# Attention with routed experts on one core: first scores ahead of the branch, a new order for stretches without expert work, new durations in the plan

## The chip, the cores and the metric

The kernel runs on one core of a Trainium2 chip. The metric is the device time of one execution in microseconds (us), the median over runs. TensorE (PE in the rows, PEld for its weight loads) multiplies matrices, ScalarE (ACT) does tanh and exponential, VectorE (DVE) the elementwise work and the casts, GpSimd (POOL) small fills and indirect transfers, and SyncE (SP) issues most DMA transfers. About 1%, 4.6 us here, is what a measurement of this kernel can tell from no change.

## What is computed

Attention over 8 batches, 12 heads, 448 places and head size 64 with capped scores, then a routed expert layer on the 128 best places of each batch:

```python
scores = scale * q @ k.T                    # (448 x 448 for each head)
scores = cap * tanh(scores / cap)           # cap = 30
attn   = softmax(scores);  x = attn @ v     # heads side by side: (8, 448, 768)

s = x[b] @ w_gate                           # for each batch b
top = the 128 places with the largest s     # each goes through the expert
out[b] = x[b]
out[b, top] += sigmoid(s[top]) * (relu(x[b, top] @ w1) @ w2)   # 768 -> 1024 -> 768
```

Everything is float32. Where more speed is wanted, a factor is split into a high and a low part and the product is made of three.

## The kernel before

The 96 heads are done four at a time, in 24 "doubles"; three doubles make a batch. A double has four units, three of 128 keys and a last one of 64. A unit of **scores** (`scores_mm`, L476) is 16 matmuls (12 where the parts are split, from the fifth double on) into the one score buffer `psS` of four PSUM banks. ScalarE takes the tanh out of `psS` into one of four `p` buffers (L911) and then the exponential in place (L918). A unit of **values** (`values_mm`, L507) is 56 matmuls from `p` and `v` into `psV`, the only accumulator, of two banks. After the last unit of a double VectorE evacuates `psV` (`evac`, L538 to L544), and the result is stored and scored for the gate (L573). The two short last units of two neighbouring doubles share one unit of scores.

When a batch has its three doubles, **selection** (`select_proc`, L589) adds the gate scores (L600), writes them to a line in DRAM (`put`, L611), reads the line back broadcast to all 128 partitions (`get`, L614), joins its tail (`sums`, L618), ranks all places by comparisons (L640, L648), makes one-hot columns (L677), and turns them into indices on TensorE (L687). A gather fetches the rows (L703, POOL), and the **expert** follows: transposes (L732), first layer, relu (L817), transposes, second layer (both L778, matmul by matmul), combination (L832), scatter (L839). Picks, transposes and both layers take the one bank pair `psT` (`K.banks`). Each selection begins behind its own batch, so that expert work is there only in some stretches.

The order of all this is worked out when the kernel is built. `Sim` holds a clock for each engine; every `Task` has an engine, a duration in ns, what it depends on and a priority, and is emitted in the order that the plan gives. On the chip each engine then goes through its instructions in that order and waits for semaphores. On TensorE `Front.policy` (L1002) chooses between Q (scores), V (values) and F (expert work): if a run of four units of values is ready, or one that continues such a run (`run_ready`), the order of choice is V, Q, F, otherwise Q, F, V. A choice that can start within 170 ns is taken, else the one that starts first. `LATE` adds time to the planned landing of the broadcast row before `sums` is placed in VectorE's order.

Ahead of a branch on the cap (L1280), `load_flag` (L319) loads the cap, makes an identity on POOL, warms TensorE up with seven products of it and tests the cap, and `first_loads` (L1148) starts the loads of the first double on SP. Loads and the flag stand outside the planned part; the fast path behind the branch is the planned one.

Of the kernel before, what the change touches and what calls it, by code (L numbers as in the profile page):

```python
# [16 lines left out]
P = 128  # L17
HD = 64
CAP_FAST = 40.0
EPS = 1e-9  # L20
WARM = 7
HALF = (slice(0, HD), slice(HD, 2 * HD))
# [3 lines left out]

LATE = 3000

# [290 lines left out]
def load_flag(tc, K, cap):  # L319
    nc = tc.nc  # L320
    nc.sync.dma_start(K.cap, cap.to_broadcast([P, 1]))
    make_identity(nc, K.ident)
# [38 lines left out]
def weights_proc(tc, K, w1, w2):  # L361
# [17 lines left out]
    for n, (nm, w, i, m) in enumerate(parts):  # L379
# [5 lines left out]
            hi, st[:, :m]), deps=[land], reads=[src], prio=K.wprio, kind="whi"))  # L385
        b = sim.add(Task("DVE", m * 1.05 + 70, lambda t, hi=hi, lo=lo, st=st, m=m:
                         nc.vector.tensor_tensor(lo, st[:, :m], hi.bitcast(F32),
# [87 lines left out]

def scores_mm(tc, K, D, c, i):  # L476
    full = K.NCH - 1
    if D.parts and c < full:
        (kh, kl), (qh, ql) = ([part[nm].slots[0].obj for part in (D.high, D.low)] for nm in "kq")
        terms = ((kh, qh), (kh, ql), (kl, qh))  # L480
        for r in range(2):
            for n, (a, b) in enumerate(terms):
                for j in range(2):
                    tc.nc.tensor.matmul(K.S4[:, 2 * r + j, :K.S],  # L484
                                        lhsT=a[HALF[j], r, c * P:(c + 1) * P],
                                        rhs=b[HALF[j], r, :], start=(n == 0), stop=(n == 2))
        return
    k, q = D.at("k"), D.at("q")
    for r in range(2):
        for h in range(2 if c < full else 1):  # L490
            for j in range(2):
                half, n = (h, 2 * r + j) if c < full else (r, 2 * i + j)
                at = c * P + h * HD
                tc.nc.tensor.matmul(K.S4[HALF[half], n, :K.S], lhsT=k[HALF[j], r, at:at + HD],  # L494
                                    rhs=q[HALF[j], r, :], start=True, stop=True)
# [27 lines left out]
def output_proc(tc, K, D):  # L523
# [24 lines left out]
    for r in range(2):  # L548
        e = Task("DVE", 790, lambda t, r=r: evac(t, r), deps=[D.values] + out,
                 take=[K.rec] if r else [K.rec, K.xn, K.xt],  # L550
# [38 lines left out]
def select_proc(tc, K, b):  # L589
# [20 lines left out]
    def put(t):  # L610
        nc.sync.dma_start(t.slots[0].obj.rearrange("o (p c) -> (o p) c", c=NCH), score)  # L611

    def get(t):
        nc.sync.dma_start(t.slots[0].obj, ln.obj.to_broadcast([P, NCH * P]))  # L614

    def sums(t):
# [6 lines left out]

    w = yield Task("SP", 700, put, deps=[t], take=[K.line], refs=[1], reads=[sc], lag=900, prio=0,
                   kind="put")
    ln = w.slots[0]
    r = yield Task("SP", 700, get, deps=[w], take=[K.row], refs=[2 * NCH], reads=[ln], lag=900,
                   prio=0, kind="get")
    rs = r.slots[0]
    row = rs.obj  # L630
    places = row.rearrange("p (a c) -> p a c", c=NCH)
    r = yield Task("DVE", 600, sums, deps=[(r, LATE)], reads=[sc], prio=1, kind="joined")
    r = [r]
    k = yield Task("DVE", 0, lambda t: None, take=[K.rk], refs=[2], prio=1, kind="none")
    rk = k.slots[0]
    todo = []
    for c in range(NCH):
        def greater(t, c=c):
# [4 lines left out]
        def ties(t, c=c):  # L643
# [7 lines left out]

        todo.append(sim.add(Task("DVE", 820, greater, deps=r, reads=[rs, sc], prio=PG,
                                 kind="greater")))
        todo.append(sim.add(Task("DVE", 430 + 110 * c, ties, deps=r, reads=[rs, sc], prio=PG,
                                 kind="ties")))
# [9 lines left out]
    for n in range(chunks):  # L665
# [3 lines left out]
        def one_hot(t, s0=s0):  # L669
            sel = t.slots[0].obj  # L670
            for c in range(NCH):
# [4 lines left out]
                else:  # L676
                    nc.vector.tensor_scalar(sel[:, c, :], K.iota, rk.obj[:, 2, c:c + 1], None,  # L677
                                            op0=ALU.is_equal)

        o = yield Task("DVE", 790, one_hot, deps=[rank], take=[K.sel], refs=[1],  # L680
                       reads=[rk] if n == chunks - 1 else [], prio=1, kind="onehot")
# [166 lines left out]
class Front:  # L848

    def __init__(self, tc, K, Ds):  # L850
# [19 lines left out]
        NB = K.B  # L870
        self.total = NB * 18800
        self.over = False

    def score_est(self):
# [14 lines left out]
    def score_task(self):  # L889
# [18 lines left out]
        def soft(_):  # L908
# [13 lines left out]
            self.S_free = th.start + 1768 + 60  # L922
            e = yield Task("ACT", 1690, exp, deps=[th], prio=3, kind="exp")
            for D, c in two:
# [77 lines left out]
    def policy(self):  # L1002
# [18 lines left out]
        seg = self.seg  # L1021
        run = self.run_ready(t)
        if run:
            order = "VQF"
        elif True:
            order = "QFV"
        else:
            order = "QVF"
        kind = None
# [4 lines left out]
        if kind is None:  # L1034
            wait = {"Q": 0, "V": 0, "F": PATIENCE}
            kind = min(start, key=lambda k: start[k] + wait[k])
        return self.commit(start[kind], f[1] if kind == "F" else None, kind, shapes[kind],
                           kind == "F" and seg != "F")

    def run_ready(self, t):  # L1040
# [106 lines left out]

def first_loads(tc, K, D):  # L1148
    nc = tc.nc
    for nm, src, ring in (("q", K.qd, K.q), ("k", K.kd, K.k), ("v", K.vd, K.v)):  # L1150
# [4 lines left out]
        setattr(D, nm, ev)  # L1155
    q, k = D.at("q"), D.at("k")
    nc.sync.dma_start(k[:, :, :2 * HD], K.kd[D.d][:, :, :2 * HD])
    for r in range(2):
        nc.sync.dma_start(q[:, r], K.qd[D.d][:, r])
    nc.sync.dma_start(k[:, :, 2 * HD:], K.kd[D.d][:, :, 2 * HD:])  # L1160
    nc.sync.dma_start(D.at("v"), K.vd[D.d])
    ones(tc, D.v, D.v)


# [97 lines left out]
def main_kernel(ctx: ExitStack, tc: tile.TileContext, q, k, v, cap, w_gate, w1, w2, out, C, dims):  # L1262
# [11 lines left out]
    K.const = ctx.enter_context(tc.tile_pool(name="const", bufs=1))  # L1274
    allocate(tc, K)
    load_flag(tc, K, cap)
    first = Double(K, 0)
    first_loads(tc, K, first)
    fast = nc.values_load(K.fast[0:1, 0:1], min_val=0, max_val=1)
# [58 lines left out]
```

## Time and profile before

| what | us |
|---|---|
| median of 3 runs (lowest to highest) | 457.3 (454.99 to 459.11) |
| the profiled execution | 458.26 |
| its span, first to last instruction | 456.5 |
| TensorE busy in the span | 431.3 (94%) |
| ScalarE busy | 303.0 (66%) |
| VectorE busy | 276.1 (60%) |
| GpSimd busy | 23.6 (5%) |

The rows come from the profiled execution. Times are microseconds from the start of the span. A matmul's end is modelled, so a busy TensorE is not one at its peak. In square brackets of a row stands how long the engine was idle before it, and what ended that.

### The profile page before, as it was taken

Reading aid. Unit: us, or ns where it says so; the run is one execution under the profiler, and the core shown is the slowest. Engines: PE = TensorE matmul, PEld = TensorE weight load, DVE = VectorE, ACT = ScalarE, POOL = GpSimd, SP = SyncE. Lnnn points to the kernel's source line nnn. Section 1 sums busy time; section 2 is a strip of 40 time slices with the busy share of each in tenths; the row PEclk is TensorE's granted clock in tenths of the full one; section 3 lists DMA queues with packets and bytes.
Section 4 is the critical chain, followed back from the end, with each engine's and each line's share of the span. In section 5 each row is a group of like instructions: output and inputs, shape, how many; then the busy total and the mean of one; then the engine's idle time right before and its main releaser. Section 6 shows DMA issues by size and latency. Waiting matters only on the chain.

```text
span 456.5 us, 17936 instructions
## 1 busy us (share of the span) xinstructions
PE 431.3 (94%) x8126; PEld 360.5 (79%) x8126; DVE 276.1 (60%) x847; ACT 303.0 (66%) x191; POOL 23.6 (5%) x55
## 2 busy tenths in 40 slices
PE   6999889999999999999999999999999799999993
PEld 4665566778889788898788988789888689878893
DVE  0176789965963874847657695479455832476211
ACT  4889989895895785876499498597678696011000
POOL 1000000100000000000000020000010000100010
PEclk9899999999999999999999999999999899999999
DMA  7977396462353532623254453522732201401011
GB/s 229 369 235 257 112 288 202 159 226 86 114 168 90 192 106 86 227 74 118 59 190 118 151 163 108 184 87 84 233 123 67 84 3 42 137 1 36 2 71 41
DMA packets 34197, 60.75 MB, mean 133 GB/s; under 512 B 11200, under 2 KB 21184, under 8 KB 34112
## 3 DMA queue, kind: packets, MB, share of 16 engines
q1 hardware_dynamic: 32832, 53.22, 35.9%
q0 software_dynamic: 1280, 6.29, 4.2%
q8 instruction: 66, 1.08, 0.9%
q14 instruction: 19, 0.16, 0.1%
HBM read 45.33 MB, written 14.17 MB: 130 GB/s over the span
## 4 chain that ended last, share of the span: by engine, by line
PE 80%; ACT 7%; DMA 5%; issue 3%; DVE 3%; SPq 1%; POOL 0%; DVEq 0%; POOLq 0%; ACTq 0%
PE psV L507 27%; PE psT L778 22%; PE psS L484 16%; PE psS L494 7%; ACT p L911 4%; PE psA L778 4%; ACT p L918 2%; PE psB L778 2%; DMA row<-line 1%; PE psT L732 1%; DMA xe<-out,idx 1%; DMA k<-in_k 1%; ACT plent L911 1%; DMA out<-p,idx 1%; DMA q<-in_q 1%
## 5 line engine op out<-in xcount | busy, mean ns | idle before, releaser
L911 ACT ACTIVATE p<-psS,sc 128x1792 f32<-128x1792 f32 x63 | 110.3, 1750 | 63.8 <-PE psS L494 34.2
L507 PEld LDWEIGHTS psV<-v,p 128*64 128x64 f32 (+1 forms) x3864 | 106.0, 139 | 23.4 <-issue 11.6
L507 PE MATMUL psV<-v,p 128*64 128x65 f32 (+1 forms) x3864 | 113.5, 225 | 5.9 <-issue 2.0
L918 ACT ACTIVATE p<-p,capc 128x1792 f32<-128x1792 f32 x63 | 112.9, 1793 | 1.7
L484 PE MATMUL psS<-qh,kh 64*128 64x448 f32 x240 | 49.1, 405 | 2.3 <-ACT p L911 2.1
L911 ACT ACTIVATE plent<-psS,sc 128x1792 f32<-128x1792 f32 x21 | 36.8, 1752 | 14.4 <-PE psS L484 7.7
L538 DVE RECIPROCAL rec<-psV 128x7 f32<-128x7 f32 x48 | 9.6, 200 | 60.0 <-PE psV L507 49.8
L494 PE MATMUL psS<-q,k 64*64 64x448 f32 x328 | 37.3, 569 | 3.9 <-ACT p L911 2.7
L918 ACT ACTIVATE plent<-plent,capc 128x1792 f32<-128x1792 f32 x21 | 37.6, 1793 | 0.7
L507 PEld LDWEIGHTS psV<-v,plent 128*64 128x64 f32 (+1 forms) x1288 | 34.8, 137 | 4.1 <-issue 2.7
L507 PE MATMUL psV<-v,plent 128*64 128x65 f32 (+1 forms) x1288 | 37.7, 223 | 0.3 <-issue 0.2
L573 DVE CUSTOM_DVE_ANT_0 jk<-xn,wg 128x256 bf16<-128x256 f32 x72 | 30.4, 422 | 1.3
L484 PEld LDWEIGHTS psS<-qh,kh 64*128 64x128 f32 x240 | 22.8, 185 | 9.0 <-ACT p L911 4.5
L539 DVE TENSOR_TENSOR xn<-psV,rec 128x384 f32<-128x384 f32 x48 | 26.8, 558 | 1.9 <-DVE rec L538 0.3
L453 DVE CAST kh<-k 128x896 fp32r<-128x896 f32 x20 | 12.5, 624 | 22.8 <-PE psS L484 22.8
L640 DVE TENSOR_SCALAR_CACHE_REDUCE jk<-row,score 128x512 bf16<-128x512 f32 (+1 forms) x32 | 23.7, 740 | 0.8
L494 PEld LDWEIGHTS psS<-q,k 64*64 64x64 f32 x328 | 11.8, 138 | 15.6 <-issue 9.0
L484 PE MATMUL psS<-ql,kh 64*128 64x448 f32 x120 | 22.3, 366 | 0.0
L778 PE MATMUL psT<-w2h,hh 64*128 64x384 f32 x192 | 21.3, 345 | 1.0 <-DVE xl L748 0.4
L484 PE MATMUL psS<-qh,kl 64*128 64x448 f32 x120 | 22.1, 363 | 0.0
L484 PE MATMUL psS<-qlent,kh 64*128 64x448 f32 x120 | 21.9, 362 | 0.0
L484 PE MATMUL psS<-qh,klent 64*128 64x448 f32 x120 | 21.9, 362 | 0.0
(149 smaller groups left out, 604.9 us busy)
## 6 DMA issues: line engine op xcount, KB each, us to landing
v<-in_v SPq DMA_DIRECT2D x23, 455.0 KB, 3.7
q<-in_q SPq DMA_DIRECT2D x22, 448.0 KB, 4.8
k<-in_k SPq DMA_DIRECT2D x22, 448.0 KB, 5.7
out<-xn SPq DMA_DIRECT2D x24, 384.0 KB, 3.5
stage<-in_moe_w SPq DMA_DIRECT2D x4, 512.0 KB, 6.0
row<-line SPq DMA_DIRECT2D x8, 256.0 KB, 3.9
stage<-in_moe_w SPq DMA_DIRECT2D x5, 384.0 KB, 3.2
out<-xt SPq DMA_DIRECT2D x48, 32.0 KB, 3.1
```

Source lines behind the costliest of these rows:

```text
L453: nc.vector.tensor_copy(t.slots[0].obj, self.at(nm))
L484: tc.nc.tensor.matmul(K.S4[:, 2 * r + j, :K.S], lhsT=a[HALF[j], r, c * P:(c + 1) * P], rhs=b[HALF[j], r, :], start=(n == 0), stop=(n == 2))
L494: tc.nc.tensor.matmul(K.S4[HALF[half], n, :K.S], lhsT=k[HALF[j], r, at:at + HD], rhs=q[HALF[j], r, :], start=True, stop=True)
L507: tc.nc.tensor.matmul(D.acc.obj[HALF[g], r, i * WIDE:(i + 1) * WIDE], lhsT=p[rows, h, n * HD:(n + 1) * HD], rhs=v[rows, u, :], start=(c == ...
L538: nc.vector.reciprocal(rec, blocks[:, :, K.D])
L539: nc.vector.tensor_tensor(slots[0].obj.rearrange("p c (r j d) -> p r j c d", r=2, j=2)[:, r], blocks[:, :2 * full, :K.D].rearrange("p (j c ...
L573: nc.vector.tensor_tensor_reduce(out=K.jk[:, :x.shape[1]], in0=x, in1=g, scale=1.0, scalar=0.0, op0=ALU.mult, op1=ALU.add, accum_out=part[ ...
L640: nc.vector.tensor_scalar(K.jk[:m], row[:m], score[:m, c:c + 1], None, op0=ALU.is_gt, op1=ALU.add, accum_out=rk.obj[:m, 0, c:c + 1])
L732: nc.tensor.transpose(t.slots[0].obj[:, h, i * HD:(i + 1) * HD], src()[half, i * P:(i + 1) * P], K.ident[half, half])
L778: ins = nc.tensor.matmul(bank.obj[:, g, :width], lhsT=pair.obj[part][HALF[h], i, :], rhs=K.wts[r][HALF[h], i, g * width:(g + 1) * width], ...
L911: nc.scalar.activation(slot.obj, K.S4[:, :, :K.S], AF.Tanh, scale=K.sc)
L918: nc.scalar.activation(slot.obj, slot.obj, AF.Exp, scale=K.cap)
```

## The change

The cap's load moves into `first_loads`, which now runs ahead of `load_flag`; half of q is loaded from ACT's queue. `first_scores` issues the first unit of scores ahead of the branch into the two bank pairs `K.acc` and `K.banks`, which are idle then. `Front.begin` plans the first tanh in two parts (one for each pair), its exponential, and ten small matmuls behind the tanh. The policy gets a test, `backlog`: if no expert product is ready within 1000 ns, the order of choice depends on what was done last (after scores F, V, Q; after values Q, F, V; after expert work V, Q, F). `put` and `get` of the first batch go to GpSimd's queue with planned costs of 1000 and 2800 ns and no `LATE`; `LATE` is halved for the others. Several planned durations are set anew, and the comparisons of the last selection get a higher priority.

```diff
-WARM = 7
+WARM, KEEP = 7, 10
-LATE = 3000
+LATE = 1500
+THIN_Q, THIN_V, THIN_F = "FVQ", "QFV", "VQF"
+SOON = 1000
+LINE, LATER, FIRST = ("POOL", 1000, 2800, "gpsimd"), ("SP", 700, 900, "sync"), 1
...
 def load_flag(tc, K, cap):
-    nc.sync.dma_start(K.cap, cap.to_broadcast([P, 1]))
...
-        b = sim.add(Task("DVE", m * 1.05 + 70, lambda t, hi=hi, lo=lo, st=st, m=m:
+        b = sim.add(Task("DVE", m * 1.05 + 145, lambda t, hi=hi, lo=lo, st=st, m=m:
...
-def scores_mm(tc, K, D, c, i):
+def scores_mm(tc, K, D, c, i, banks=None):
+    if banks is None:
+        banks = [K.S4[:, n] for n in range(4)]
...
-        e = Task("DVE", 790, lambda t, r=r: evac(t, r), deps=[D.values] + out,
+        e = Task("DVE", 1030, lambda t, r=r: evac(t, r), deps=[D.values] + out,
...
+    eng, busy, lag, queue = LINE if b < FIRST else LATER
+    queue = getattr(nc, queue)
...
-    r = yield Task("DVE", 600, sums, deps=[(r, LATE)], reads=[sc], prio=1, kind="joined")
+    r = yield Task("DVE", 860, sums, deps=[(r, LATE if eng == "SP" else 0)], reads=[sc], prio=1, kind="joined")
+    pg = .5 if K.tail else PG
...
-        o = yield Task("DVE", 790, one_hot, deps=[rank], take=[K.sel], refs=[1],
+        o = yield Task("DVE", 1000, one_hot, deps=[rank], take=[K.sel], refs=[1],
...
+    def begin(self):
+        K, sim, nc = self.K, self.sim, self.tc.nc
+        D, c = self.work[0][0]
+        self.u = 1
+        pairs = [r.free.pop() for r in (K.acc, K.banks)]
+        for s in pairs:
+            s.refs = 1
+        def tanh(t):
+            for r, s in enumerate(pairs):
+                nc.scalar.activation(t.slots[0].obj[:, 2 * r:2 * r + 2], s.obj[:, :, :K.S], AF.Tanh,
+                                     scale=K.sc)
+            D.P[c], D.pslot[c] = t.slots[0].obj, t.slots[0]
+        def exp(t):
+            x = th.slots[0].obj
+            nc.scalar.activation(x, x, AF.Exp, scale=K.cap)
+        def warm(t):
+            for _ in range(KEEP):
+                nc.tensor.matmul(t.slots[0].obj[:, 0, :HD], lhsT=K.ident[HALF[0]],
+                                 rhs=K.ident[HALF[0], :HD], start=True, stop=True)
+        th = sim.add(Task("ACT", 2000, tanh, take=[K.p], refs=[1], reads=pairs, prio=0,
+                          kind="tanh"))
+        D.exp[c] = sim.add(Task("ACT", 1740, exp, deps=[th], prio=0, kind="exp"))
+        w = Task("PE", KEEP * 111, warm, deps=[th], take=[K.banks], refs=[1], prio=(0, 0),
+                 kind="warm")
...
-            e = yield Task("ACT", 1690, exp, deps=[th], prio=3, kind="exp")
+            e = yield Task("ACT", 1740, exp, deps=[th], prio=3, kind="exp")
...
-        run = self.run_ready(t)
-        if run:
-            order = "VQF"
-        elif True:
-            order = "QFV"
+        if not self.backlog(t, SOON):
+            order = THIN_Q if seg == "Q" else THIN_V if seg == "V" else THIN_F
         else:
-            order = "QVF"
+            order = "VQF" if self.run_ready(t) else "QFV"
...
+    def backlog(self, t, within):
+        for task in self.sim.pend["PE"]:
+            if task.kind in ("open", "mm"):
+                if task.kind == "open" and self.K.open >= 1:
+                    continue
+                r = task.ready()
+                if r is not None and r <= t + within:
+                    return True
+        return False
...
-def first_loads(tc, K, D):
+def first_loads(tc, K, D, cap):
...
+    nc.scalar.dma_start(q[:, 0], K.qd[D.d][:, 0])
+    nc.sync.dma_start(K.cap, cap.to_broadcast([P, 1]))
     nc.sync.dma_start(k[:, :, :2 * HD], K.kd[D.d][:, :, :2 * HD])
-    for r in range(2):
-        nc.sync.dma_start(q[:, r], K.qd[D.d][:, r])
+    nc.sync.dma_start(q[:, 1], K.qd[D.d][:, 1])
     nc.sync.dma_start(k[:, :, 2 * HD:], K.kd[D.d][:, :, 2 * HD:])
     nc.sync.dma_start(D.at("v"), K.vd[D.d])
     ones(tc, D.v, D.v)
+
+def first_scores(tc, K, D):
+    pairs = K.acc.slots[0].obj, K.banks.slots[0].obj
+    scores_mm(tc, K, D, 0, 0, [b[:, n] for b in pairs for n in range(2)])
+    for s in (D.q, D.k):
+        s.slots[0].refs -= 1
...
+    first = Double(K, 0)
+    first_loads(tc, K, first, cap)
     load_flag(tc, K, cap)
-    first = Double(K, 0)
-    first_loads(tc, K, first)
+    first_scores(tc, K, first)
     fast = nc.values_load(K.fast[0:1, 0:1], min_val=0, max_val=1)
```

## Rows read from the trace of the kernel before

**Rows 1.** Page, busy us (share of the span) and instructions of each engine.

```profile
PE 431.3 (94%) x8126; PEld 360.5 (79%) x8126; DVE 276.1 (60%) x847; ACT 303.0 (66%) x191; POOL 23.6 (5%) x55
```

**Rows 2.** Windows: start:end, length, busy us by engine; last granted clock, DMA share, GB/s.

```profile
0.00:20.00 20.00, 16.26 (x190) 9.81 (x190) 1.01 (x8) 12.00 (x8) 3.30 (x18) 0.91 0.85 292
20.00:100.00 80.00, 73.13 (x1636) 53.38 (x1634) 63.39 (x170) 74.01 (x45) 1.91 (x6) 1.00 0.67 220
100.00:350.00 250.00, 246.28 (x4836) 212.97 (x4834) 164.69 (x510) 186.30 (x115) 12.44 (x24) 1.00 0.41 130
350.00:370.00 20.00, 17.41 (x424) 14.93 (x422) 15.45 (x55) 12.91 (x10) 0.13 (x1) 0.91 0.16 49
370.00:450.00 80.00, 78.24 (x1054) 69.43 (x1053) 30.81 (x105) 17.79 (x18) 4.84 (x5) 1.00 0.14 42
450.00:456.50 6.50, 0.00 (x0) 0.00 (x0) 0.76 (x2) 0.00 (x0) 0.96 (x1) 0.83 0.18 67
```

**Rows 3.** Timeline 0 to 15 us: start, us, engine, line, operation.

```profile
0.81 0.39 SPq L321 DMA_DIRECT2D capc<-in_cap  x1
1.42 3.35 PE L325 MATMUL psT<-ident 128*128 128x128 f32 x14 [1.42 <-POOL ident masks.py:199]
2.01 1.06 SPq L1159 DMA_DIRECT2D q<-in_q  x2
3.64 0.14 DVE L328 RECIPROCAL sc<-capc 128x1 f32<-128x1 f32 x1
3.75 0.14 DVE L327 TENSOR_SCALAR fast<-sq 1x1 int32<-1x1 f32 x1
5.08 2.70 PE L494 MATMUL psS<-q,k 64*64 64x448 f32 x16 [0.30 <-DMA q<-in_q]
7.90 1.75 ACT L911 ACTIVATE p<-psS,sc 128x1792 f32<-128x1792 f32 x1 [3.77 <-PE psS L494]
9.23 0.12 POOL L473 MEMSET v<- 128x14 f32 x1 [7.86 <-DMA v<-in_v]
9.69 1.79 ACT L918 ACTIVATE p<-p,capc 128x1792 f32<-128x1792 f32 x1
9.71 2.54 PE L494 MATMUL psS<-q,k 64*64 64x448 f32 x16 [1.92 <-ACT p L911]
12.32 1.75 ACT L911 ACTIVATE p<-psS,sc 128x1792 f32<-128x1792 f32 x1 [0.84 <-PE psS L494]
```

**Rows 4.** A window at the start, columns as in rows 2.

```profile
9.70:12.20 2.50, 2.49 (x18) 0.65 (x18) 0.53 (x3) 1.78 (x1) 2.07 (x7) 0.66 0.99 378
```

**Rows 5.** The chain that ended last: start, us, what it was.

```profile
25.59 1.73 PE psS L494 x16
...
263.63 0.97 PE psV L507 x56
...
349.93 6.03 PE psV L507 x224
...
360.82 1.29 issue
...
373.69 1.78 PE psV L507 x56
```

**Rows 6.** Timeline of ScalarE: a wait for scores.

```profile
32.27 1.76 ACT L911 ACTIVATE p<-psS,sc 128x1792 f32<-128x1792 f32 x1 [1.30 <-PE psS L494]
```

**Rows 7.** Selection: timeline of SP and VectorE, and the page's issue of the gathers.

```profile
57.80 0.69 SPq L611 DMA_DIRECT2D line<-score  x1
60.02 0.55 DVE L384 CAST w2h<-stage 128x768 fp32r<-128x768 f32 x1
71.07 0.28 DVE L618 TENSOR_TENSOR row<-row 128x64 f32<-128x64 f32 x1
...
253.11 0.28 DVE L618 TENSOR_TENSOR row<-row 128x64 f32<-128x64 f32 x1 [1.61 <-DMA row<-line]
...
xe<-out,idx POOLq DMA_INDIRECT x6, 4.6
```

More of the change, by code (lines that the diff above doesn't have):

```diff
@@ L483, in scores_mm @@
                 for j in range(2):
-                    tc.nc.tensor.matmul(K.S4[:, 2 * r + j, :K.S],
+                    tc.nc.tensor.matmul(banks[2 * r + j][:, :K.S],
                                         lhsT=a[HALF[j], r, c * P:(c + 1) * P],
@@ L493, in scores_mm @@
                 at = c * P + h * HD
-                tc.nc.tensor.matmul(K.S4[HALF[half], n, :K.S], lhsT=k[HALF[j], r, at:at + HD],
+                tc.nc.tensor.matmul(banks[n][HALF[half], :K.S], lhsT=k[HALF[j], r, at:at + HD],
                                     rhs=q[HALF[j], r, :], start=True, stop=True)
@@ L610, in put @@
     def put(t):
-        nc.sync.dma_start(t.slots[0].obj.rearrange("o (p c) -> (o p) c", c=NCH), score)
+        queue.dma_start(t.slots[0].obj.rearrange("o (p c) -> (o p) c", c=NCH), score)
     def get(t):
-        nc.sync.dma_start(t.slots[0].obj, ln.obj.to_broadcast([P, NCH * P]))
+        queue.dma_start(t.slots[0].obj, ln.obj.to_broadcast([P, NCH * P]))
     def sums(t):
@@ L622, in sums @@
                                        accum_out=score[:HD, last:])
-    w = yield Task("SP", 700, put, deps=[t], take=[K.line], refs=[1], reads=[sc], lag=900, prio=0,
+    eng, busy, lag, queue = LINE if b < FIRST else LATER
+    queue = getattr(nc, queue)
+    w = yield Task(eng, busy, put, deps=[t], take=[K.line], refs=[1], reads=[sc], lag=lag, prio=0,
                    kind="put")
     ln = w.slots[0]
-    r = yield Task("SP", 700, get, deps=[w], take=[K.row], refs=[2 * NCH], reads=[ln], lag=900,
+    r = yield Task(eng, busy, get, deps=[w], take=[K.row], refs=[2 * NCH], reads=[ln], lag=lag,
                    prio=0, kind="get")
@@ L650, in ties @@
                                            accum_out=rk.obj[:m, 1, c:c + 1])
-        todo.append(sim.add(Task("DVE", 820, greater, deps=r, reads=[rs, sc], prio=PG,
+        todo.append(sim.add(Task("DVE", 820, greater, deps=r, reads=[rs, sc], prio=pg,
                                  kind="greater")))
-        todo.append(sim.add(Task("DVE", 430 + 110 * c, ties, deps=r, reads=[rs, sc], prio=PG,
+        todo.append(sim.add(Task("DVE", 430 + 110 * c, ties, deps=r, reads=[rs, sc], prio=pg,
                                  kind="ties")))
@@ L871, in __init__ @@
         self.total = NB * 18800
+        self.begin()
         self.over = False
+    def begin(self):
[22 more added lines that the diff above has]
+                 kind="warm")
+        w.reads.append(lambda: w.slots[0])
+        sim.add(w)
     def score_est(self):
```

## The prediction

> **What bounds the kernel now.** I read the page's busy shares first. TensorE is busy 94% of the span, no other engine over 66% [rows 1]. So the question is where the missing 25.2 us lie. The table of windows answers it: TensorE is idle 3.7 us of the first 20, 6.9 us between 20 and 100, 3.7 us in the 250 between 100 and 350, 2.6 us between 350 and 370, 1.8 us between 370 and 450, and all of the last 6.5 us, where only the last combination and scatter run [rows 2]. A change of order can win only from those holes, and the last 6.5 us is not touched by it.
>
> Then the timeline of the start. The first scores wait for q (issued third on SP) until 5.08, the first tanh starts at 7.90, and the second scores wait until that tanh has left the one score buffer, 9.71 [rows 3]. TensorE does nothing for 1.92 us ahead of them, and in the stretch that follows the granted clock is 0.66 on average, between its two levels of 1.2 and 2.4 GHz, so that 16 matmuls take 2.54 us where the same 16 take 1.73 later [rows 3, 4, 5]. ScalarE, which feeds everything in this stage, starts its second tanh at 12.32.
>
> Between 20 and 100 both engines are nearly full: ScalarE 74.0 of 80 us, TensorE 73.1 [rows 2]. Here the chain of waits jumps between them. Where two units of values stand together, the next scores come late and ScalarE waits 1.30 us [rows 6]. The same happens at about 59 and 85 us, so there are three such places. The worst place is at 350: four units of values in a row take 6.03 us, in which ScalarE gets no scores, and soon after TensorE itself waits 1.29 us because no exponential is ready [rows 5].
>
> **The change, part by part.** *First scores ahead of the branch.* Half of q is issued on ACT, so it need not wait behind the cap and k on SP: q was issued at 2.01 and its first half was there at 5.08, 3.1 us later [rows 3]. Issued near 0.9 (SP's own first transfer goes out at 0.81) it lands at about 4.0, before TensorE has ended its 14 warming matmuls at 1.42 + 3.35 = 4.77 [rows 3]. The first 8 matmuls then run from 4.8 to about 5.7. The other half of q moves one place forward and is there at about 5.0, so the second 8 end near 6.7. Tanh in two parts: half of 1.75 us with some 0.1 for the second start, so it runs 5.8 to 7.8, and the exponential of 1.79 to 9.6. The second scores go to the score buffer, which nobody holds. They need the rest of k, which is issued earlier than before, and they run about 6.8 to 8.6. So the second tanh starts at 9.6 where it started at 12.32: **-2.7 us**. At worst q and k land as before; then only the split tanh and the free buffer count: second part of tanh from 7.9 to 8.8, exponential to 10.6, -1.7. At best the lost clock does not fall either, which is 2.54 - 1.73 = 0.8 more: -3.5. The ten small matmuls put behind the second scores stand in a time in which TensorE waits for the exponential, so I cost them at nothing; without that cover they are some 1 us (the plan's own 111 ns each).
>
> *Scores first where no expert work is ready.* In thin stretches the new order alternates scores and values, where the old one took values as long as they were ready. No work goes away. Bounded by the holes: between 20 and 100 from 0 to -6.9 us of idle TensorE, and the three late scores are 1.30 us of ScalarE each. Since both engines are nearly full there, I take half of three such waits, **-1.9**. At 350 the expert's first layer has just ended and its second is not ready, so the run of four would be broken up and the 1.29 us wait filled: **-1.3** (0 to -2.6, the hole of that window). Between 100 and 350: **-0.6** of the 3.7 us. The price is more changes of array shape: one large unit alone takes 1.78 on the chain, a small one 0.97, so three large and one small are 6.31 where a run of the four takes 6.03, which is 0.09 for each joint [rows 5]. I count 35 joints in the timeline of values, 9 of them in thin stretches: **+0.8** (if all 35 break, +3.2).
>
> *First selection on POOL's queue.* Between the issue of the score line (57.80) and the first use of the returned row (71.07) lie 13.3 us [rows 7]. The plan now has 2 times (1000 + 150 + 2800 ns) = 7.9 us, so the first expert starts about 5 us earlier beyond the shift. Nothing of TensorE's work is saved; experts only fill time in which TensorE is idle 6.9/80 = 9%: **-0.5** (0 to -1.2). The nearest rows for a POOL transfer are the gathers, 4.6 us from issue to landing [rows 7]: two of these are 9.2, 1.3 late. What would wait is VectorE, because the row's first use now has no margin in the plan, and behind it the evacuation of values. A VectorE wait of that size stands in the trace, 1.61 us at 253.11, and TensorE lost nothing in it, since its run of values covered it [rows 2, 7]. So 0, at most +1.3.
>
> By the Trainium skill, "SBUF — State Buffer", section SBUF: two separate sides, a POOL-issued DMA cannot write its descriptors while VectorE runs an fp32 copy in its two-port mode. VectorE's weight casts of 0.55 us stand in that stretch [rows 7]; by the rule each of the two transfers could be held by one, 1.1 us, which would take the selection's -0.5 to -0.4. No run here shows it yet.
>
> *Durations.* Longer plan costs (exponential 1690 to 1740 against 1.79 measured, evacuation 790 to 1030) add no work; they move the plan's clock nearer to the chip's and reorder everything behind. I take 0, with 2.6 us to either side, the largest hole that an order has made after 100 [rows 2]. The shorter margin LATE for later rows takes 1.5 us from a wait that occurred once in eight: 0 to +1.5, taken as 0. In the tail the ranking goes ahead of other VectorE work; TensorE is idle only 1.8 us in 370 to 450 [rows 2]: 0, at most 0.7 either way.
>
> **Sum:** -2.7 - 1.9 - 1.3 - 0.6 + 0.8 - 0.5 = **-6.2 us**. The profiled execution took 458.26 (span 456.5 and 1.8 around it), which becomes 452.1. The median of the runs, 457.3, lies 1.0 below that execution; the same sum from there gives **451.1**, which is my figure.
>
> **Rivals.** (1) *Only the start counts.* Values put off in thin stretches must be paid when TensorE is full, and the holes between 20 and 100 come from the single score buffer and the evacuation, which stay. Then -2.7 - 0.5 + 0.8 = -2.4 and 454.9. For it: ScalarE and TensorE are both above 91% there. Against: the 1.29 us wait at 350, which order alone made. (2) *The start gets slower.* The loads now stand in the code ahead of the identity, and with them POOL's write of ones into v, which waited for v until 9.23; the warming matmuls wait for the identity, which is POOL's too [rows 3]. If POOL kept code order, the identity would be ready near 9.8 instead of 1.4, the 14 warming matmuls end at 13.2, the first scores (2.5 us) let the first tanh half go at 14.5, and the second tanh starts at 18.3, 6.0 late. Then 457.3 + 6.0 - 3.5 = 459.8, slower than before; it decides as soon as the start comes 6.2 us later than I have it, and it comes 8.7 later. Against it: ahead of the branch the engines do not keep code order, since VectorE's reciprocal (L328) ran before L327 [rows 3]. (3) *Joints.* If the new test finds "no expert work" inside expert phases too, all 35 joints break: -2.7 + 3.2 = +0.5, and 457.8. Against: inside a layer the next product is ready at once, so the test finds it. (4) *The first scores come no earlier* because q's half waits behind the table load on ACT: -1.7 for the start, -5.2 in all, 452.1; this lies within my forecast.
>
> **Chances.** Forecast with (4), 445.5 to 454: 0.62. Only the start: 0.20. Slow start: 0.07. Joints: 0.06. Something else in the new order that costs over 5 us: 0.05. The bounds of the terms reach from -12 (445.3) to about +0.2 (457.5), and beyond the latter lie the slow start, most of the joints and the last case, under 2 in 10: range **445.5 to 457.5**; the likeliest case alone has 447 to 454. About 1%, 4.6 us, is what a measurement of this kernel can tell from no change. Faster by more than that takes nine tenths of the forecast, 0.56, and a tenth of the second case: 0.58. Slower by over 1% means over 461.9: half of the slow start and the last case: 0.08. Within 1%: 0.34.
>
> **What would show it.** The second tanh near 9.6, no granted clock below 1 before 20 us, no wait of ScalarE over 1 us for scores before the first expert, no run of four values at the end of the fifth expert's first layer, the first row used some 8 to 9 us after its line was issued. I am wrong if TensorE's idle time after 20 us stays near 14 us (rival 1), if warming starts after 9 us (rival 2), or if values units alone become the rule in expert phases (rival 3).

## The result, and the profile after

The changed kernel takes 462.0 us in the median of 20 runs (458.49 to 466.3), the kernel before in the same comparison 457.65 (454.99 to 459.87). The ratio is 1.009, 95% interval 1.0067 to 1.0114: slower by 0.9%, some 4 us, where I forecast 451.1. (The comparisons leave disturbed runs out.)

The first view of the kernel after is the table of windows that answers to [rows 2]: stretch, its length, then busy us and number of instructions of TensorE, its weight loads, VectorE, ScalarE and POOL, granted clock, DMA share, GB/s.

```profile
core 0 of [0], span 460.4 us
0.00:20.00 20.00, 15.29 (x206) 10.47 (x210) 1.01 (x8) 11.57 (x9) 3.30 (x18) 1.00 0.86 285
20.00:100.00 80.00, 71.02 (x1543) 50.99 (x1537) 58.60 (x151) 65.64 (x39) 2.97 (x7) 0.96 0.59 192
100.00:350.00 250.00, 245.19 (x4790) 212.83 (x4788) 163.34 (x508) 181.67 (x110) 12.44 (x23) 0.99 0.42 133
350.00:370.00 20.00, 19.91 (x446) 18.31 (x448) 12.73 (x40) 14.80 (x10) 1.77 (x2) 1.00 0.27 82
370.00:450.00 80.00, 78.94 (x1148) 68.54 (x1142) 40.27 (x142) 29.20 (x24) 4.98 (x6) 1.00 0.17 53
450.00:460.40 10.40, 3.19 (x38) 2.87 (x34) 1.14 (x2) 0.00 (x0) 0.96 (x1) 0.79 0.12 44
```

Against [rows 2], TensorE's idle time is 1.0 us longer in the first 20 us (4.71), 2.1 longer between 20 and 100 (8.98), 1.1 longer up to 350 (4.81), 2.5 shorter between 350 and 370 (0.09), 0.7 shorter up to 450 (1.06) and 0.7 longer behind that (7.21). Over the span it is 460.4 - 433.5 = 26.9 us against 25.2. TensorE's busy time is 433.5 us where it was 431.3 [rows 1]; the twenty small matmul passes take 2.44 of that. So the hole at 350 was closed, and other stretches lost more than that. Between 20 and 450 the idle time adds up to 14.94 us in both kernels: the change moved the holes and did not make them smaller. ScalarE, which the new order was to feed earlier, is busy 65.64 us of the 80 between 20 and 100, where it was 74.01.

The start, from the timeline of TensorE and ScalarE after (start, duration, engine, line, operation, and in brackets the idle time before it and its end):

```profile
4.71 1.77 PE L501 MATMUL psV<-q,k 64*64 64x448 f32 x8 [4.71 <-DMA k<-in_k]
6.41 2.95 PE L330 MATMUL psT<-ident 128*128 128x128 f32 x14
6.59 1.01 ACT L895 ACTIVATE p<-psV,sc 128x896 f32<-128x896 f32 x1 [1.81 <-PE psV L501]
9.29 0.98 PE L501 MATMUL psT<-q,k 64*64 64x448 f32 x8
10.34 1.01 ACT L895 ACTIVATE p<-psT,sc 128x896 f32<-128x896 f32 x1 [2.74 <-PE psT L501]
11.71 2.44 PE L905 MATMUL psT<-ident 64*128 64x64 f32 x20
11.89 1.75 ACT L953 ACTIVATE p<-psS,sc 128x1792 f32<-128x1792 f32 x1 [0.55 <-PE psS L501]
16.91 1.74 ACT L953 ACTIVATE p<-psS,sc 128x1792 f32<-128x1792 f32 x1
```

The 14 warming matmuls (L330), which ran from 1.42 while the loads were under way [rows 3], now stand between the two halves of the first scores. TensorE idles until 4.71, does one half, then warms up, and only then does the other half. ScalarE waits 2.74 us between its two halves. The second unit's tanh starts at 11.89, 0.43 earlier than before; the third at 16.91, where it started at 16.54.

Between 60 and 100, TensorE after by windows of 10 us (busy, granted clock, DMA share, GB/s), and rows of its timeline, one of them from 150, with a row of ScalarE at the end:

```profile
60.00:70.00 10.00, 7.69 (x150) 1.00 0.86 291
70.00:80.00 10.00, 9.69 (x198) 0.83 0.40 127
80.00:90.00 10.00, 7.26 (x182) 0.86 0.74 253
90.00:100.00 10.00, 10.00 (x189) 0.96 0.28 79
```

```profile
69.32 0.47 PE L491 MATMUL psS<-qh,kh 64*128 64x448 f32 x2 [1.85 <-ACT plent L953]
71.39 2.87 PE L514 MATMUL psV<-v,p 128*64 128x65 f32 x56 [0.20 <-issue]
87.61 0.90 PE L742 MATMUL psT<-ident,xe 64*128 64x64 f32 x12 [1.47 <-DMA xe<-out,idx]
88.44 2.88 PE L514 MATMUL psV<-v,p 128*64 128x65 f32 x56
91.16 1.80 PE L514 MATMUL psV<-v,plent 128*64 128x65 f32 x56
150.87 0.58 PE L742 MATMUL psT<-ident,xe 64*128 64x64 f32 x12 [2.42 <-DMA xe<-out,idx]
94.43 1.76 ACT L953 ACTIVATE p<-psS,sc 128x1792 f32<-128x1792 f32 x1 [6.26 <-PE psS L491]
```

TensorE waits 1.85 us for a tanh, then the granted clock falls, and a unit of values takes 2.87 us instead of 1.85. At 87.61 the transposes of the first expert's rows (L742) stand at the head of TensorE's queue and wait for their gather, with values and scores behind them. Two units of values (2.88 and 1.80 us, the first at a low clock: the window from 80 to 90 shows 0.86) come ahead of the next scores, which ScalarE gets only at 94.43, after 6.26 us without work. The same kind of wait comes back at 150.87, 2.42 us.

### The profile page after: what moved, and what is told of

The parts are those of the page before. It is cut to its first block, busy times and chain, and to the rows that moved or that the text cites. A ratio compares the mean times of both kernels' runs of the same rounds, so it can differ in the third digit from the quotient of the medians.

```text
span 460.4 us, 17976 instructions
## 1 busy us (share of the span) xinstructions
PE 433.5 (94%) x8146; PEld 364.0 (79%) x8146; DVE 277.1 (60%) x849; ACT 302.9 (66%) x190; POOL 26.4 (6%) x57
## 4 chain that ended last, share of the span: by engine, by line
PE 82%; DMA 6%; ACT 5%; issue 3%; DVE 3%; POOL 0%; SPq 0%; POOLq 0%; DVEq 0%
PE psV L514 29%; PE psT L788 21%; PE psS L491 16%; PE psS L501 6%; PE psV L788 3%; ACT p L953 2%; DMA xe<-out,idx 2%; PE psB L788 2%; ACT p L960 2%; DMA stage<-in_moe_w 1%; PE psT L742 1%; ACT plent L953 1%; DMA p<-out,idx 1%; DMA k<-in_k 1%; DVE w1l L392 1%
## 5 line engine op out<-in xcount | busy, mean ns | idle before, releaser
L953 ACT ACTIVATE p<-psS,sc 128x1792 f32<-128x1792 f32 x62 | 108.6, 1752 | 69.9 <-PE psS L501 35.7
L960 ACT ACTIVATE p<-p,capc 128x1792 f32<-128x1792 f32 x62 | 111.2, 1793 | 1.8
L501 PE MATMUL psS<-q,k 64*64 64x448 f32 x312 | 34.1, 546 | 1.8 <-ACT p L953 1.1
L788 PE MATMUL psT<-w1h,xh 64*128 64x512 f32 x144 | 20.4, 402 | 0.8 <-issue 0.2
```

The costliest lines, as they stand in the source:

```text
L501: tc.nc.tensor.matmul(banks[n][HALF[half], :K.S], lhsT=k[HALF[j], r, at:at + HD], rhs=q[HALF[j], r, :], start=True, stop=True)
L788: ins = nc.tensor.matmul(bank.obj[:, g, :width], lhsT=pair.obj[part][HALF[h], i, :], rhs=K.wts[r][HALF[h], i, g * width:(g + 1) * width], ...
L953: nc.scalar.activation(slot.obj, K.S4[:, :, :K.S], AF.Tanh, scale=K.sc)
L960: nc.scalar.activation(slot.obj, slot.obj, AF.Exp, scale=K.cap)
```

## The experiments

The prediction's parts were first made alone, each on the kernel before. Ratios are to the kernel before on the same chip; 0.01 is some 4.6 us. The kernels ran on several chips, so different runs are compared by their ratios and not by their medians.

**Each part alone.** The edit is a part of the diff above without the rest: s_start has the moved loads, `first_scores` and `begin`; s_thin has `backlog`, `SOON` and the three orders; s_sel has `LINE`, `LATER`, `FIRST` and `LATE`; s_dur has the five planned durations and `pg`.

> Start alone (loads and first scores ahead of the branch, split first tanh, ten small matmuls); order, selection, margin and durations as before. My prediction costed it at -2.7 us. In the trace of the whole change the first half of the scores stands on TensorE ahead of the 14 warming matmuls and the second half behind them, so that the second tanh starts at 11.9 instead of 12.3 and the third later than before. Theory START (the misplaced warming matmuls eat the gain): 0 to +1.5 us against before, second tanh within 0.5 us of before's 12.3, TensorE idle about 1 us more in the first 20 us. Rival (the start is as predicted and the loss lies elsewhere): -2 to -3 us.

> The new order for thin stretches alone. Predicted -1.9 -1.3 -0.6 +0.8 = -3.0 us. Theory ORDER-GOOD: -2 to -3, with the hole of TensorE between 350 and 370 gone (2.6 us before, 0.1 with the whole change). Rival ORDER-COST (scores taken first leave TensorE waiting for tanh and values piled behind, as at 67 us of the whole change): +1 to +3, TensorE's idle time of 20 to 100 us above before's 6.9.

> First selection on POOL's queue, the margin LATE 3000 to 1500 (0 for the first batch); nothing else. Predicted -0.5 us (0 to -1.2 for the earlier selection, 0 to +1.5 for the margin, up to +1.3 for a late row). Theory MARGIN (the margin also covered the gather; without it the transposes of the gathered rows come to the head of TensorE's queue too early and block it, after which the granted clock falls): +2 to +4 us, TensorE waits of 1 to 2.5 us at the transposes (the line of the 128-column transposes) in the first or second batch. Rival (the waits of the whole change come from the planned durations): -1 to +0.5, no such wait over 0.5 us.

> The planned durations alone (exponential 1740, evacuation 1030, selection vector rows 860 and 1000, combination +75 ns, ranking first in the tail). Predicted 0 with 2.6 to either side. Theory DURATIONS (the longer evacuation moves values behind scores that still wait for a tanh): +1 to +3 us. Rival (the plan's clock only comes nearer to the chip's): 0 to -1.

| part alone | median | ratio (95%) | forecast for the part |
|---|---|---|---|
| start | 461.57 | 1.0067 (1.0038 to 1.0095) | -2.7 us |
| thin order | 460.31 | 1.0017 (0.9988 to 1.0047) | -3.0 |
| selection and LATE | 459.92 | 1.0030 (1.0005 to 1.0055) | -0.5 |
| durations, ranking first in the tail | 469.02 | 1.0225 (1.0180 to 1.0271) | 0 (2.6 to either side) |

None gains. The start costs 3 us, the durations 10; together the four make +3.4%, while the whole change costs 0.9%. So the parts do not add, and the part with the largest price is the one that I had taken as nothing. None of the four came out as I expected before the run. Theory START has the mechanism of s_start (the second tanh at 12.89, TensorE idle 4.80 us in the first 20 instead of 3.74), but the price is twice its 1.5. s_thin and s_sel lie between theory and rival, s_sel with a wait of 1.77 us at the second expert's transposes (150.30), such as theory MARGIN names. s_dur costs over three times the most that theory DURATIONS allowed.

**The start.** The warming matmuls wrote into the bank pair of the second half of the scores. Here they write in turn into both pairs, so both halves must follow them:

```diff
-    warm = K.banks.slots[0].obj[:, 0]
-    for _ in range(WARM):
+    for i in range(WARM):
+        warm = (K.acc, K.banks)[i % 2].slots[0].obj[:, 0]
```

s_startw is the start alone with this edit, m_warm the whole change with it.

> Start alone as in s_start, but with the 14 warming matmuls writing in turn to the two bank pairs that the first scores use, so that they stand ahead of both halves of these scores. Theory START: the misplaced warming matmuls were the term that my prediction of -2.7 us lacked; then the second tanh starts near 10 instead of 12.3 and the time is 2 to 4 us under s_start, -0.5 to +1 against before (the ten small matmuls still cost what they cost). Rival (time gained at the start is not kept, since the first 100 us wait for something else, or the ten small matmuls delay the rest): within 1 us of s_start although the second tanh comes 1.5 to 2 us earlier.

> The whole change with the warming matmuls ahead of both halves of the first scores, nothing else. Theory START: -2 to -4 us against the changed kernel. Rival: less than 1 us, because the places at 67 to 90 us and 146 us, where TensorE waits for a tanh and for a gather, stay as they are and set the time.

s_startw: 457.51 us, 0.9971 (0.9951 to 0.9990). m_warm: 457.24 us, 0.9986 (0.9955 to 1.0016). Against the same kernels with the misplaced warming that is 0.9971/1.0067 = -1.0% and 0.9986/1.009 = -1.0%, some 4.5 us in both, more than the 2 to 4 that I expected. The timeline of s_startw shows a start near the one forecast:

```profile
1.43 0.80 PE L330 MATMUL psV<-ident 128*128 128x128 f32 x2 [1.43 <-POOL ident masks.py:199]
4.15 0.64 PE L330 MATMUL psV<-ident 128*128 128x128 f32 x2
6.56 1.01 ACT L895 ACTIVATE p<-psV,sc 128x896 f32<-128x896 f32 x1 [2.03 <-PE psV L501]
7.47 1.00 ACT L895 ACTIVATE p<-psT,sc 128x896 f32<-128x896 f32 x1
8.81 1.75 ACT L953 ACTIVATE p<-psS,sc 128x1792 f32<-128x1792 f32 x1 [0.35 <-PE psS L501]
13.83 1.74 ACT L953 ACTIVATE p<-psS,sc 128x1792 f32<-128x1792 f32 x1
```

Warming ends at 4.79, about when the loads are there (4.71 in the kernel after). The second tanh starts at 8.81; it stands ahead of the first exponential, where I had it behind, so the third is the one to compare: 13.83 where it was 16.54, 2.7 us earlier. The edit changes nothing but the banks that the warming writes, and with them the order on TensorE ahead of the branch, so that the misplaced warming costs these 4.5 us is shown. Of the 2.7 us about 1.3 are left at the end (0.9971).

The ten small matmuls, left out of s_startw:

```diff
-        sim.add(w)
```

> s_startw without the ten small matmuls (20 passes, 2.44 us in the traces) behind the second scores. My prediction costed them at nothing. Theory COVERED: within 0.7 us of s_startw. Rival COST: 1 to 2.5 us faster than s_startw, because the third scores and the first values came later by them. Rival CLOCK: slower than s_startw, with a granted clock under 1 between 10 and 20 us as before had.

455.47 us, 0.9962 (0.9939 to 0.9984), which does not differ from s_startw within the intervals. TensorE in the first 20 us, first in s_startw, then in w_nokeep:

```profile
0.00:20.00 20.00, 18.37 (x266) 1.00 0.86 292
```

```profile
0.00:20.00 20.00, 16.13 (x250) 1.00 0.86 292
```

It is busy 2.24 us less and idle so much more: they lie in time that TensorE waits through anyway. Nor does the clock fall without them.

**The thin order, freed from a wait.** In s_thin the hole at 350 is gone (19.48 us busy of 20 there), but TensorE waits 2.74 us at the second expert's transposes, at 146. w_thin is the thin order on the mended start, w_thin_g the same with a longer planned lag of the gathers, w_g that lag without the thin order:

```diff
-                       reads=[idx], lag=2600, prio=1, kind="gather"))
+                       reads=[idx], lag=4200, prio=1, kind="gather"))
```

> Mended start (warming matmuls ahead of both halves of the first scores) with the new order for thin stretches; selection, margin and durations as before. s_startw gave 457.5 (0.9971 of before), s_thin 1.0017. My prediction for these parts was -2.7 and -3.0. Theory ADD: 0.9988 of before, that is -0.5 us. Rival (with the start in order the thin order's gain at 350 us is kept): -2 to -4 us, the fastest kernel so far; the hole of 2.6 us between 350 and 370 gone and no wait over 1 us at the transposes of gathered rows.

> w_thin (0.9969 of before) with the planned lag of the gathers of rows 2600 made 4200 ns. Theory GATHER: the wait of 2.4 us at the transposes of the second expert's rows at 140 us goes and the gain is kept, 1.5 to 3 us under w_thin (0.990 to 0.994 of before). Rival (the idle time moves to another place, as g_after did against the changed kernel): within 1 us of w_thin, no wait at these transposes but others instead.

> s_startw (0.9971 of before) with the planned lag of the gathers 4200 instead of 2600 ns, order in thin stretches as before. Theory ORDER FREED (the gain belongs to the thin order, which without the lag is eaten by the wait for the gather): within 1 us of s_startw, since its trace has no wait of TensorE at the transposes of gathered rows. Rival LAG (the longer lag helps by itself): 0.988 to 0.992, like w_thin_g (452.0).

| kernel | median | ratio (95%) |
|---|---|---|
| s_startw | 457.51 | 0.9971 (0.9951 to 0.9990) |
| w_thin: with the thin order | 456.18 | 0.9969 (0.9949 to 0.9989) |
| w_g: with the lag | 456.84 | 0.9970 (0.9938 to 1.0001) |
| w_thin_g: with both | 452.03 | 0.9886 (0.9847 to 0.9925) |

On the mended start neither edit gains by itself; together they gain 0.8%, 3.8 us, and the intervals do not touch. (w_thin came out between theory ADD and its rival, w_g as theory ORDER FREED has it.) The rows that decide, POOL's and TensorE's timelines of w_thin:

```profile
136.07 1.00 POOL L849 DMA_INDIRECT out<-xe,idx  x1 [8.67 <-DVE xe L842]
139.92 1.73 POOL L713 DMA_INDIRECT xe<-out,idx  x1 [2.86 <-DVE gt L725]
144.69 0.59 PE L742 MATMUL psT<-ident,xe 64*128 64x64 f32 x12 [2.39 <-DMA xe<-out,idx]
```

and of w_thin_g:

```profile
120.62 1.16 POOL L713 DMA_INDIRECT xe<-out,idx  x1 [10.43 <-DVE gt L709]
144.31 1.01 POOL L849 DMA_INDIRECT out<-xe,idx  x1 [0.98 <-DVE score L607]
144.29 0.53 PE L742 MATMUL psT<-ident,xe 64*128 64x64 f32 x12
```

In w_thin the second expert's gather goes out 3.85 us behind the first expert's scatter, and its transposes wait for it. With the longer lag the plan issues the gather 19 us earlier, ahead of the scatter, and the transposes, at the same time as in w_thin, find their rows. So the lag did not move the transposes back; it changed the order of two transfers. The busy times on the two pages, w_thin first (span 454.3 us), then w_thin_g (449.8), show what that is worth:

```profile
PE 431.3 (95%) x8146; PEld 360.8 (79%) x8146; DVE 275.9 (61%) x848; ACT 303.0 (67%) x191; POOL 25.0 (6%) x55
PE 429.1 (95%) x8146; PEld 360.7 (80%) x8146; DVE 275.6 (61%) x847; ACT 303.1 (67%) x192; POOL 23.8 (5%) x55
```

TensorE's idle time falls by 2.3 us, from 23.0 to 20.7, about the one wait of 2.39. The other 2.2 us are busy time with the same number of matmuls; where they come from is not shown. Over all 20 kernels (the 18 here, before and after) the wait goes with this order without exception: in the eight where the second gather is issued behind the first scatter (after, s_thin, s_sel, b_evac, m_warm, u_dur, w_thin, u_start), TensorE waits 1.3 to 2.9 us at these transposes, in the twelve others not at all. The time does not follow from it alone, though: s_dur and u_thin, two of the slowest, are among the twelve. That a gather behind a scatter must wait for the scatter to land is likely, since both touch the output, the scatters land in 3.1 us in the median, and in w_thin the indices were ready at 137.93, 2.0 us before the gather went out; it was not tried by itself.

In the whole change the same lag did not help:

> The whole change with the planned lag of the gathers of rows 2600 ns made 4200, near the 4.7 to 5.3 us that the traces show. Theory MARGIN: TensorE's waits at the transposes of gathered rows (1.5 us at 87.6, 2.4 us at 146) go, and with them the stretches of lower clock behind them; -3 to -5 us against the changed kernel. Rival (the waits are a sign and not a cause: the plan only puts the same idle time elsewhere): within 1.5 us, with other waits in the same stretch.

464.94 us, 1.0129 (1.0089 to 1.0169). The waits at the transposes are gone, as theory MARGIN said, and the time is no shorter (by the ratios 1.8 us longer, with intervals that overlap): the rival, about. TensorE's idle time between 100 and 350 rose from 4.81 to 7.48 us in other places.

**The durations.** Which of them costs, on the kernel before:

```diff
-        e = Task("DVE", 790, lambda t, r=r: evac(t, r), deps=[D.values] + out,
+        e = Task("DVE", 1030, lambda t, r=r: evac(t, r), deps=[D.values] + out,
```

b_exp has instead the one line of the exponential, `Task("ACT", 1690, exp, ...)`, at 1740.

> The kernel before with one planned duration changed: the evacuation of one half of the values 790 to 1030 ns, which is what the trace of before shows (reciprocal 200 + product 558 + last 64 columns 275 = 1033 ns). Theory EVACUATION: of the +10.5 us of all the durations together it is nearly the whole, +6 to +10, although this number is nearer to the chip than 790. Rival (the five durations act together, or the selection's and the combination's carry it): +2 or less.

> The kernel before with the exponential planned at 1740 instead of 1690 ns (measured 1.79 us), nothing else. Theory EVACUATION: within 1.5 us of before, since a uniform 50 ns per unit of ScalarE only stretches the plan. Rival (the plan is so touchy that any 3% edit moves the end by several us): more than 3 us to either side, and then the parts' figures say little about the parts.

b_evac: 467.35 us, 1.021 (1.0176 to 1.0245). b_exp: 457.36 us, 1.0009 (0.9990 to 1.0029). The evacuation is nearly the whole price, although 1030 is what the trace of before has, in its groups by line (busy us, mean ns; 200 + 558 + 275 = 1033):

```profile
L539 DVE TENSOR_TENSOR xn<-psV,rec 128x384 f32<-128x384 f32 x48 | 26.8, 558 | 1.9 <-DVE rec L538 0.3
L544 DVE TENSOR_SCALAR xt<-psV,rec 128x64 f32<-128x64 f32 x48 | 13.2, 275 | 0.0
L538 DVE RECIPROCAL rec<-psV 128x7 f32<-128x7 f32 x48 | 9.6, 200 | 60.0 <-PE psV L507 49.8 <-PE psT L778 10.2
```

Where it goes in b_evac, by the windows of TensorE and two rows of its last expert:

```profile
140.00:150.00 10.00, 7.34 (x140) 0.89 0.42 135
150.00:160.00 10.00, 9.86 (x116) 0.77 0.17 29
230.00:240.00 10.00, 8.24 (x171) 0.83 0.79 242
```

```profile
445.89 1.06 PE L732 MATMUL psA<-ident,hs 64*128 64x64 f32 x16 [0.79 <-DVE hs L817]
447.75 2.60 PE L778 MATMUL psT<-w2h,hh 64*128 64x384 f32 x16 [0.79 <-DVE hh L518]
```

The busy times of b_evac, from its page:

```profile
PE 435.5 (94%) x8126; PEld 362.4 (78%) x8126; DVE 276.6 (59%) x848; ACT 302.8 (65%) x190; POOL 23.7 (5%) x55
```

Its span is 465.6 us, 9.1 longer than before; TensorE is idle 30.1 us instead of 25.2 and busy 435.5 instead of 431.3 with the same number of matmuls. So 4.9 us are waits and 4.2 us are matmuls that take longer. That the lower clock behind the waits does this fits the windows above and the mean granted clocks (0.978 to 0.985 in its six executions, 0.984 to 0.995 in those of the kernel before beside them), but no run sets the two apart. Part of both lies at the end: attention ends 14.4 us later than before (403.3 against 388.9), the last gather goes out at 430.89 instead of 414.41, and the last expert stands alone on TensorE, its waits uncovered.

**One part undone in the whole change.** The same four parts of the diff, each taken back in the changed kernel. Idle time of TensorE and the end of attention (the end of its last values) are those of each kernel's own trace.

> The whole change with the start of before. Theory START (misplaced warming matmuls cost 3 us, s_start +3.1, m_warm 4.8 under the changed kernel): 458 to 459.5. Theory INTERACTION: outside of 456 to 462.

> The whole change with the order of before in thin stretches. Theory FIXED PRICES (s_thin's +0.8): about 461, 1 us under the changed kernel. Theory INTERACTION (parts only have prices inside a plan; long planned evacuations are what cost, and the thin order repairs them): 466 to 473. By the theory TAIL (the last scatter comes 53 us or more after the end of attention) the slow case shows attention ending after 403 us and the last gather after 430.

> The whole change with the selection's queue and margins of before (SP, 3000). Theory FIXED PRICES (s_sel's +1.4): 460 to 461. Theory MARGIN (the shorter margin causes the waits for gathers): 457 to 459, no wait over 1 us at the transposes of gathered rows. Theory INTERACTION: anywhere from 455 to 470, and no nearer to FIXED PRICES than chance.

> The whole change with the planned durations and the ranking's priority of before. Alone these durations cost +10 us (s_dur, 469.0). Theory DURATIONS: they cost here too, so this is 3 to 10 us under the changed kernel (452 to 459). Rival (the new order and the selection on POOL's queue already take back what the durations cost, as the parts' sum of +3.1, +0.8, +1.4 and +10.5 us against the whole's +4.2 suggests): within 2 us of the changed kernel.

| undone in the whole change (1.009) | median | ratio (95%) | idle 100 to 350 | attention ends |
|---|---|---|---|---|
| start | 461.41 | 1.0085 (1.0049 to 1.0121) | 5.62 | 400.0 |
| thin order | 469.63 | 1.0277 (1.0228 to 1.0327) | 12.21 | 399.2 |
| selection and LATE | 459.91 | 1.0051 (1.0024 to 1.0077) | 3.63 | 391.6 |
| durations | 471.46 | 1.0274 (1.0247 to 1.0301) | 7.47 | 409.9 |

The durations cost 10 us alone and save 8.5 here (1.0274 against 1.009); the thin order is worth nothing alone and 8.5 us here. My expectation for u_dur failed on both sides: neither did the time fall, nor did it stay within 2 us. The start of before is no faster here than the misordered one, against theory START; only the mended one is. u_sel lies between the two figures expected, 1.8 us under the changed kernel by the ratios with intervals that overlap, and the waits over 1 us at the transposes are gone, as theory MARGIN said. Theory TAIL, that slow kernels share a late end of attention and a last gather after 430, falls: u_thin is slow with an end at 399.2 and a last gather at 422.5. Its time lies in many waits between 100 and 350.

**The fastest.** w_thin_g without the ten small matmuls:

> w_thin_g (452.0) without the ten small matmuls. Theory COVERED: 450.5 to 453, within 1.2 us of w_thin_g. Rival COST: 449 to 450.5, the full 2.4 us that they take.

452.05 us, 0.9844 (0.9803 to 0.9885); the median is that of w_thin_g, on another chip. The ratio is 0.4% lower with intervals that overlap, so it stays open whether the small matmuls cost something here. Both are faster than the two kernels of this study, the kernel before by 5.4 and 6.6 us by the medians. They take the start (mended) and the thin order from the change, the lag of the gathers from the experiments, and leave its durations and its selection out.

## Why the prediction was wrong, point by point

**First scores, -2.7.** The failed step is "before TensorE has ended its 14 warming matmuls at 4.77": I had the first scores behind the warming because the code has them there, though I had noted in rival (2) that engines ahead of the branch do not keep code order. I looked for that danger on POOL, where the identity came in time, and not on TensorE. The half of the scores that writes into another bank pair than the warming passed it. Mended, the step has the size that I gave it, with the second tanh ahead of the first exponential: the third tanh comes 2.7 us earlier, of which 1.3 are kept at the end. In the whole change the mended start is worth 4.8 us (1.009 against 0.9986). So of the 11 us between forecast and result somewhat under half is this step; the rest of the change, forecast to gain 3.5, brought nothing. The clock did not fall to 0.66 as in [rows 4]: the window from 10 to 20 shows 1.00 in either order. The ten small matmuls at nothing: right where they were left out alone (w_nokeep), with the cover that I named.

**Thin order, -1.9 - 1.3 - 0.6 + 0.8 = -3.0.** Measured 0 alone, -3.8 where the gather is issued in time. The hole at 350 went as forecast: 0.09 us idle where it was 2.59. Not for my reason, though: a run of four values still stands after it at 363.8, but no wait follows it. Runs were not broken up as a rule: counted in the timelines of values, the kernel before has 33 joints (I had 35), s_thin 35 and the kernel after 36, so the +0.8 had nothing to price. What I had no term for was what is late next: experts now take the time that attention had, in s_thin the first scatter comes 11 us earlier (137.29 against 148.78) and the second gather 14 later (141.16 against 127.10), so that they change places. The -1.9 failed too: the waits of ScalarE over 1 us did not go (of the three that I had at 1.30, the one at 85 was 0.88 before); the one of 6.26 us after is longer than any that I had listed in that stretch.

**First selection, -0.5.** Measured +0.3% alone, with LATE. The line was issued at 59.41 and the row first used at 69.81, 10.4 us instead of the 13.3 of [rows 7], where I had 8 to 9: as the dear case I took the 4.6 us of a gather for each of the two transfers, and on POOL's queue the line took 3.1 from issue to landing and the row 6.9. VectorE waited 0.59 us for it, inside my bound of 1.3. The first gather went out 4.3 us earlier than before, and the first expert still started at the same time (94.22 against 94.75): its transposes waited 1.47 us, and two units of values, the first at a low clock, and one of scores, 5.7 us in all, came between them and its first product. What failed is to carry "TensorE lost nothing in it" over to the new plan: a margin shortened in the plan moves all the transfers behind it, and one of them stood at the head of TensorE's queue. By the Trainium skill, "TensorE: Matmul & The Clock Gate", section The mechanism, matmuls start and end in program order. The trace agrees: at 87.61 and 150.87 everything behind the transposes stands still with them. Whether VectorE's casts held POOL's two transfers, the rule that I weighed there, no run tells apart.

**Durations, 0.** The mis-sized term: +10.5 alone, of which the evacuation makes nearly all, -8.5 inside the whole; my bound was 2.6 to either side. I had bounded it by the largest hole that an order had made. But the plan chooses greedily, so that one duration moves every later choice, and the losses come as many small waits; in b_evac 4.2 us more busy time came with them.

**The rivals.** None came true as written. The mark that I had given for rival (1), idle time after 20 us staying near 14, is there (14.94 us in both kernels), but its figure, 454.9, was a gain. Rival (2) had the place, the start, but another engine. (3) Joints did not decide: there are no fewer than before. By the ratio the change lies just within 1%, to which I had given 0.34, but on the side that I had thought least likely and outside the range. With the warming in order it would have been 457.24 (m_warm), just inside the upper edge of the range; that would have been luck, since neither the thin order nor the durations came out as I had them.

**Still open:** why the thin order and the durations are worth 8.5 us each in the whole and 0 and -10 alone. The tables show that it is so, and that part of the time goes into waits between 100 and 350 with no common place.

## What to carry to other kernels

Ahead of a planned part, read each engine's real order from the trace: an instruction that is meant to run in idle time goes there only if something makes the others wait for it, as a shared bank did here. In a plan that is made greedily, a part has no price of its own and truer durations are no gain by themselves; measure parts alone and undone, and fix the one wait that the trace names rather than the model as a whole. When work is moved earlier, look for the transfer that is overtaken, and whether an in-order queue will stop at what needs it.

## What the runs showed of the hardware that was not expected

Waits on TensorE may cost more than their length: in b_evac 4.9 us more idle time went with 4.2 us more busy time for the same matmuls, with a granted clock of 0.77 to 0.89 in the windows around and behind a wait of 1.90 us at 146. It is not shown as a rule: the wait of 2.39 us at 144.69 in w_thin was followed by a clock of 1.00. A score line written by POOL took 2.70 us from the end of its issue until the next transfer could start, and the row that came back another 6.4 us to its first use. From issue to landing the row took 6.9 us there, against a median of 3.8 for the seven rows that SP's queue fetched in the same kernel.
